# A decode attention block and its gradients: first wq chunk and third wo tile loaded at the turn between the passes, new homes for some gradient rows, another plan for the end

## The chip, the cores and the metric

The kernel runs on one core of a Trainium2 chip. The metric is the device time of one execution in microseconds; a comparison between two kernels is made from their medians. The core has five engines with a queue each: TensorE (PE, with its weight loads shown apart as PEld), VectorE (DVE), ScalarE (ACT), GpSimd (POOL) and SyncE (SP). Sixteen DMA engines move data between the device memory and the on-chip memory; transfers are issued from the queues of SP, ACT and POOL.

## The reference: what is computed

One token goes through an adaptive-layernorm block (a modulation vector made from `c` and `w_mod`), attention with a cache of 8192 keys and values for each of 32 heads of width 192, and a small mixer MLP. Then all gradients are taken with respect to ten of its inputs.

```python
mod = (_silu(c) @ w_mod).reshape(c.shape[0], 6, 1, -1)      # sa, ca, ga, sb, cb, gb
h = _layernorm(x) * (1 + ca) + sa
q = (h @ wq).reshape(B, Sq, Hq, Dh)                         # 640 -> 32 x 192
p = softmax(einsum(q, k) * Dh ** -0.5); o = einsum(p, v)
x = x + ga * (o @ wo)                                       # 6144 -> 640
h = _layernorm(x) * (1 + cb) + sb
x = x + gb * _B_ref(h, w1, w2, w3, w4)                      # w3: 640 x 1536, w4: 1536 x 640
out, vjp = jax.vjp(f, x, k_cache, v_cache, wq, wo, w3, w4, c, w_mod); grads = vjp(grad_out)
```

K and V are 100 MB each and are read (V twice), and their gradients dK and dV, 100 MB each, are written. Beside them stand the weights and their gradients: wq and dwq (640 x 6144), wo and dwo (6144 x 640), w_mod and its gradient (640 x 3840), and those of w3 and w4. All of these weight gradients are outer products of two vectors.

## The kernel before, in words

The forward pass runs over the heads: scores from K and q, softmax, the sums of V. It ends at about 530 us. Then comes the turn: the last head, the output projection, the MLP forward and backward, and the vector `dao`, from which the gradient of every head's output follows. The backward pass then runs 64 steps s = 0 to 63, two per head (half a head's 8192 positions each), from the last head down. A step multiplies a half of V by the head's gradient (DVE, L1094), sums over the width on PE (L1113), forms dS (L1459), writes dK (DVE, L1129) and dV (PE L1124, ACT L1125), and stores both from POOL (L1414, L1410), 1536 KB each. One half of V (1536 KB) is loaded per step from SP (L328), five steps ahead. dV and dK are built in a ring of five buffers (`OB`: KC, VB2, QT, KE, KD; QT is the memory of `qs_bc`), so each waits until the store five buffers earlier has landed; in the last steps V buffers that are no longer needed join the ring.

Every engine's order is the order of the program text: nothing is reordered. Into the 64 steps the smaller work is woven by a plan written by hand. `at(s0, n, g)` puts the next n pieces of a generator g at s0, s0 + 0.25, and so on; s0 is counted in steps, and each step has four slots (`slot()`, behind the second dV group, between the halves of dK, behind the sixth dV group, and at its end). At a slot every due piece is issued, in the order of the sorted plan. The pieces that matter here:

- `g_ld(n)` loads wo tile TL - n (TL = 15, 480 KB, L203) from SP into one of two buffers of tag `wo`. The load waits until the tile that had this buffer is finished, its store included.
- `g_do(n)` transposes that tile (two pieces, PE L903 and ACT L904, into the one buffer of tag `wT`) and forms the gradient of two heads' outputs (third piece, L1056). `g_dwo(n)` overwrites the tile with the rows of dwo (DVE, three instructions, L1257) and stores it from POOL.
- `g_dq(t)` and `g_wm(n)` work on chunks of wq and w_mod: a chunk is 960 KB and is worked on in two halves of five pieces (transposes, a small product, ten outer-product rows on DVE, L1216). The rows of the gradient overwrite the chunk, and the second half stores it (L1227). `next_w()` (L1154) loads the next chunk from SP in the last piece of a first half, in turn into `w_st` (the memory of `w4b`) and `stg`, one buffer each.
- `g_dw3(lo, n)` builds rows of the gradient of w3 in `stg` from `du_bc`, which lies in `w4b`, and stores them; `g_bcast` makes `dao_bc` and `du_bc`; `g_small` does small sums, one output among them.
- `put(out, w, hold)` stores at once or, for the two last wo tiles and the two last w_mod chunks, keeps the store back until a `g_held` piece (L1231).
- The twelve rows of the gradient of w4 (160 KB each) come from `dw4_act` (ACT, L962) and `dw4_dve` (DVE, L950) and are stored by `dw4_store` (POOL, L953), rows 0 to 4 from `dw4s` (part of `w4b`), the others from `stg`.

SP takes its waits in order too: while a load waits for its buffer, every load behind it stands. The order on SP at the turn is: V for s = 4, the eight-kilobyte load `er0` (L367), wo tile TL - 1, the second `er` load, then the two halves of V for s = 5 (L1424).

Of the kernel before, what the change touches and what calls it, by code (L numbers as in the profile page):

```python
# [20 lines left out]
def kernel(  # L21
# [1024 lines left out]
    stg0 = bst.tile([P, ND * CW], BF16, name="stg")  # L1046
# [19 lines left out]
    wo_l[TL - 1] = load_wo(TL - 1)  # L1066
# [11 lines left out]
    dw4_act(stg0, 5, 5, 6)  # L1078
# [6 lines left out]
    dw4_dve(stg0, 5, 6, 7)  # L1085
    dw4_store(stg0, 5, 2)
# [55 lines left out]
    cur = {}  # L1142
# [3 lines left out]
    def next_w():  # L1146
        if wseq:
            view, n = wseq.pop(0)
            if cur.setdefault("n", 0) % 2 == 0:
                w = wst.tile([P, ND, CW], BF16, name="w_st", tag="w", bufs=1)  # L1150
            else:
                w = bst.tile([P, ND, CW], BF16, name="stg")
# [32 lines left out]
    def g_chunk(b, first, v3, rows, dst, n, acc, lay):  # L1185
# [31 lines left out]
        if first:  # L1217
            next_w()
# [34 lines left out]
    def g_dwo(n):  # L1253
        t = TL - n
        w = wo_l.pop(t)
# [24 lines left out]

    def g_dw3(lo, n):
# [4 lines left out]
        if lo == 0:  # L1286
            dw4_dve(o3[:, n * F : n * F + D], 11, 11, 12)
            dw4_store(o3[:, n * F : n * F + D], 11, 1)
        nc.gpsimd.dma_start(out=dw3_v[:, lo : lo + n, :], in_=o3[:, 0 : n * F].rearrange("p (a r) -> p a r", a=n))
        if lo + n == ND:  # L1290
            next_w()
        yield
# [30 lines left out]
    at(2.0, 1, d)  # L1323
    at(2.25, 3, g_bcast(dao, ND, dao_bc))
    at(3.0, 1, g_dwo(0))
    at(4.75, 1, g_ld(2))
    d = g_do(2)
    at(6.0, 1, d)
    at(6.0, 2, d)
    at(6.5, 1, g_dwo(1))  # L1330
    at(6.75, 4, g_bcast(du, NF, du_bc))
    at(7.75, 1, g_dw3(0, 2))
    at(8.0, 1, g_ld(3))
    at(8.25, 2, g_small())
    at(8.75, 1, g_dwo(2))
    at(9.0, 3, g_do(3))
    at(9.75, 1, g_dw3(2, 2))
    at(10.0, 1, g_dwo(3))
    at(10.75, 1, g_ld(4))
    at(11.25, 1, g_dw3(4, 1))  # L1340
    at(13.0, 3, g_do(4))
    at(13.75, 1, g_dwo(4))
    for n in range(5, NT):
        d = DO0 + CWS * (n - 5) if n < NT - 2 else 47.75 + 0.75 * (n - NT + 2)
        at(d - 3.25, 1, g_ld(n))
# [3 lines left out]
    k, t = 0, TL  # L1349
    while t >= 0 or late:  # L1350
        if t >= 0 and not (late and k % 3 == 2):
            wseq.append((wq_v, t // 2))
            at(CW0 + CWS * k, 5, g_dq(t))
            at(CW0 + CWS * k + 1.25, 5, g_dq(t - 1))
            t -= 2
        else:
            wseq.append((wm_v, late[0]))
            at(CW0 + CWS * k, 10, g_wm(late.pop(0)))
        k += 1
    at(CW0 + CWS * k - 1.0, 2, g_finish_x())  # L1360
    for n in range(GX):
        wseq.append((wm_v, n))
        at(CW0 + CWS * k, 10, g_wm(n))
        k += 1
    at(CW0 + CWS * k - 1.0, 1, g_finish_c())
    for s0 in (60.25, 60.75, 61.25, 62.25):
        at(s0, 1, g_held())
# [58 lines left out]
    mul_q(0, 0)  # L1426
    load_v5(0, JQ)
# [19 lines left out]
    dw4_act(stg0, 5, 7, 11)  # L1447
# [4 lines left out]
    for s in range(NS):  # L1452
# [61 lines left out]
        if s == 0:  # L1514
            dw4_store(stg0[:, 2 * D : 6 * D], 7, 4)
# [60 lines left out]
```

## Time and profile before

| | |
|---|---|
| time, median of 3 runs | 1389.81 us (1385.27 to 1391.85) |
| the profiled execution: its own time | 1386.39 us |
| its span, first to last instruction | 1384.6 us |
| busy: PE, DVE, ACT, POOL | 83%, 80%, 66%, 8% |
| data moved by DMA | 569.38 MB |
| mean granted TensorE clock | 0.741 |

The profile is of one execution. A windows row gives start and end, its length, the busy time of PE, PEld, DVE, ACT and POOL with their counts of instructions, the granted TensorE clock (1 is full), the mean busy share of the 16 DMA engines, and the rate in GB/s. A row of a timeline gives the start, the duration, the engine (SPq is the DMA queue of SP), the line in the kernel, the operation, what is written and read, the count and, in brackets, how long the engine was idle before and what ended that. A row of a source line or tile gives the count, the least, median and largest duration in ns, and the first and last start. A waits row gives who waited for whom: total us, times, longest. The page's rows of DMA issues give the count, the size of one and the median time from issue to landing.

### The profile page before, as it was taken

What the parts mean: (1) busy time and instruction counts of PE and PEld (TensorE: products, weight loads), DVE (VectorE), ACT (ScalarE), POOL (GpSimd) and SP (SyncE); (2) the same over time, 40 slices, a digit from 0 to 9 for tenths busy, and PEclk for the clock granted to TensorE, in tenths of its full rate; (3) what the DMA queues carried; (4) which work ended last, traced back from release to release, by engine and by line L of the source; (5) the groups of instructions that cost most, each with busy time, mean ns of one, the idle gap of its engine ahead of it and who ended that gap; (6) DMA issues with size and microseconds to landing.
All of it is one profiled execution on the core that took longest, in us unless ns stands there. A gap on an engine that the chain in (4) does not pass through costs nothing.

```text
span 1384.6 us, 30509 instructions
## 1 busy us (share of the span) xinstructions
PE 1154.0 (83%) x12712; PEld 733.4 (53%) x12712; DVE 1109.2 (80%) x1455; ACT 911.1 (66%) x2007; POOL 108.6 (8%) x197
## 2 busy tenths in 40 slices
PE   3898989999998989987867977698778886987974
PEld 2777777777777777633323434343334442533421
DVE  4999999999999999986757677686677866876784
ACT  0777777777777778866545656576556665755754
POOL 0000000000000000111100111011101110110011
PEclk8999999999999999765556556565565555655555
DMA  9999999999999999799999999999999999999989
GB/s 383 396 423 425 424 416 423 413 426 418 424 413 425 415 414 380 252 416 424 422 422 425 426 414 426 426 419 425 426 422 425 417 426 384 419 425 426 422 365 378
DMA packets 76889, 569.38 MB, mean 411 GB/s; under 512 B 7439, under 2 KB 25215, under 8 KB 37199
## 3 DMA queue, kind: packets, MB, share of 16 engines
q1 hardware_dynamic: 51594, 342.03, 60.1%
q0 software_dynamic: 24640, 224.89, 38.7%
q8 instruction: 99, 1.62, 0.4%
q10 hardware_dynamic: 516, 0.51, 0.1%
q14 instruction: 40, 0.32, 0.1%
HBM read 340.97 MB, written 226.44 MB: 410 GB/s over the span
## 4 chain that ended last, share of the span: by engine, by line
issue 44%; DVE 25%; DMA 14%; PE 9%; POOL 5%; ACT 2%; POOLq 0%; SPq 0%; ACTq 0%; DVEq 0%
DVE prod L333 10%; DMA KB<-in_A_k_cache_dram 9%; DVE prod L337 5%; DVE vs L403 4%; DMA out_dram<-qs_bc 3%; PE mp L425 2%; POOL out_dram L1414 2%; POOL out_dram L1410 2%; PE half_ps L343 2%; DMA out_dram<-KB 1%; PE mp L430 1%; POOL out_dram L1227 1%; DVE pq L1094 1%; PE dot_ps L1113 1%; DVE S_h L347 1%
## 5 line engine op out<-in xcount | busy, mean ns | idle before, releaser
L1113 PE MATMUL dot_ps<-pq,ident_bf 128*128 128x256 bf16 x1494 | 365.1, 385 | 27.0 <-DVE dP L347 25.5
L410 ACT ACTIVATE vs<-VB,Ef 128x192 bf16<-128x192 bf16 x840 | 303.6, 447 | 0.0
L1125 ACT CAST KB<-dv_ps 128x768 bf16<-128x768 f32 x312 | 241.4, 805 | 83.5 <-PE dv_ps L1124 82.4
L1113 PEld LDWEIGHTS <-ident_bf 128*128 128x128 bf16 x1494 | 147.1, 121 | 172.8 <-issue 137.1
L333 DVE TENSOR_TENSOR prod<-KB,qs_bc 128x6144 bf16<-128x6144 bf16 x62 | 207.9, 3353 | 24.1 <-DMA KB<-in_A_k_cache_dram 16.6
L1124 PE MATMUL dv_ps<-do_r,er_b 1*128 1x192 bf16 x2016 | 220.9, 327 | 4.3 <-ACT KB L1125 2.8
L1129 DVE TENSOR_TENSOR KB<-qh,dS 128x3072 bf16<-128x3072 bf16 x74 | 128.1, 1753 | 95.3 <-DMA out_dram<-KB 76.4
L425 PE MATMUL mp<-vs,KB 128*128 128x193 bf16 x1984 | 188.6, 246 | 4.5 <-ACT vs L410 2.6
L425 PEld LDWEIGHTS <-KB 128*128 128x128 bf16 x1984 | 168.2, 97 | 13.6 <-DMA KB<-in_A_k_cache_dram 5.3
L904 ACT COPY wT<-wT_ps 128x1024 bf16<-128x1024 bf16 x82 | 79.2, 966 | 106.2 <-PE wT_ps L903 105.8
L1124 PEld LDWEIGHTS <-er_b 1*128 1x128 bf16 x2016 | 68.7, 103 | 141.2 <-issue 138.2
L343 PE MATMUL half_ps<-prod,ident_bf 128*128 128x256 bf16 x744 | 95.1, 279 | 44.0 <-DVE prod L337 43.9
L403 DVE TENSOR_TENSOR vs<-VB,E 128x1728 bf16<-128x1728 bf16 x120 | 123.7, 1052 | 0.3 <-ACT vs L410 0.3
L1094 DVE TENSOR_TENSOR pq<-VB,do_r 128x3072 bf16<-128x3072 bf16 x66 | 115.5, 1750 | 0.0
L337 DVE TENSOR_TENSOR prod<-prod 128x3072 bf16<-128x3072 bf16 x62 | 108.7, 1754 | 1.0
L1094 DVE TENSOR_TENSOR pq<-KB,do_r 128x3072 bf16<-128x3072 bf16 x62 | 108.5, 1750 | 0.0
L343 PEld LDWEIGHTS <-ident_bf 128*128 128x128 bf16 x744 | 72.8, 100 | 62.4 <-issue 53.5
L430 PE MATMUL mp<-vs,KB 128*64 128x193 bf16 x1968 | 105.7, 250 | 0.0
L1125 ACT CAST VB<-dv_ps 128x768 bf16<-128x768 f32 x96 | 74.7, 804 | 39.0 <-PE dv_ps L1124 38.7
L1125 ACT CAST qs_bc<-dv_ps 128x768 bf16<-128x768 f32 x104 | 80.1, 805 | 23.7 <-PE dv_ps L1124 23.2
L390 ACT ACTIVATE E<-S_h,negm 128x256 bf16<-128x256 f32 x31 | 15.7, 508 | 114.5 <-DVE negm L561 112.2
L430 PEld LDWEIGHTS <-KB 128*64 128x64 bf16 x1968 | 78.8, 109 | 19.8 <-issue 19.5
(380 smaller groups left out, 1209.4 us busy)
## 6 DMA issues: line engine op xcount, KB each, us to landing
VB<-in_A_v_cache_dram SPq DMA_DIRECT2D x93, 1536.0 KB
out_dram<-KB POOLq DMA_DIRECT2D x74, 1536.0 KB, 17.2
KB<-in_A_k_cache_dram SPq DMA_DIRECT2D x63, 1536.0 KB
KB<-in_A_v_cache_dram SPq DMA_DIRECT2D x29, 1536.0 KB
out_dram<-qs_bc POOLq DMA_DIRECT2D x25, 1536.0 KB, 17.9
out_dram<-VB POOLq DMA_DIRECT2D x25, 1536.0 KB, 17.7
wo_st<-in_A_wo_dram SPq DMA_DIRECT2D x31, 480.0 KB
w_st<-in_A_wq_dram SPq DMA_DIRECT2D x12, 960.0 KB
```

What stands on the lines that cost most here:

```text
L333: V_.tensor_tensor(out=prod, in0=src, in1=vec[:, None, :].to_broadcast([P, JH, DH]), op=ALU.mult)
L337: V_.tensor_tensor(out=prod[:, :, 0:HW], in0=prod[:, :, 0:HW], in1=prod[:, :, DH - HW : DH], op=ALU.add)
L343: T_.matmul(ps, lhsT=ident_bf, rhs=prod[:, :, k : k + TF], start=(k == 0), stop=(k == w - TF))
L403: V_.tensor_tensor(out=vs[:, 0:n, 0:DH].rearrange("p j (a b) -> p j a b", b=4), in0=v[:, v0 : v0 + n, :].rearrange("p j (a b) -> p j a b", ...
L410: A_.activation(out=vs[:, k, 0:DH], in_=v[:, v0 + k, :], func=ACT.Copy, scale=Ef[:, j0 + k : j0 + k + 1])
L425: T_.matmul(mp[:, 0:MW], lhsT=kb[:, j0 + k, 0:P], rhs=vs[:, k, 0:MW], start=(q == 0 and k == 0), stop=(z and k == JQ - 1), skip_group_chec ...
L430: T_.matmul(mp[p0 : p0 + 64, MO : MO + MW], lhsT=kb[:, j0 + k, P:DH], rhs=vs[:, k, 0:MW], start=False, stop=(z and k >= JQ - 2), skip_grou ...
L1094: V_.tensor_tensor(out=pq[:, q], in0=v_l[s][:, q * JQ : (q + 1) * JQ, :], in1=do_of(ht(s)[0])[:, None, :].to_broadcast([P, JQ, DH]), op=AL ...
L1113: T_.matmul(ps[:, q * JQ : (q + 1) * JQ, :], lhsT=ident_bf, rhs=pq[:, q, :, k : k + TS], start=(k == 0), stop=(k == w - TS), skip_group_ch ...
L1124: T_.matmul(ps[:, b, k * DH : (k + 1) * DH], lhsT=er[p0 : p0 + 1, 2 * m + k, :], rhs=doh[p0 : p0 + 1, :], start=True, stop=True)
L1125: A_.copy(out=dV4[:, 2 * q : 2 * q + 2, m * PW : (m + 1) * PW], in_=ps[:, :, 0:PW])
L1129: V_.tensor_tensor(out=dK[:, lo:hi, :].rearrange("p j (a b) -> p j a b", b=4), in0=qh.rearrange("p (a b) -> p a b", b=4)[:, None, :, :].to ...
```

## The change

It moves transfers and pieces of work; what is computed and how many bytes are moved stays as it is.

- Wo tile TL - 2 is loaded at the turn, right ahead of tile TL - 1; `g_ld(2)` is gone. So that its buffer is free, dwo(0) is built in `dw4s` and no longer in the tile TL.
- The first chunk of wq (chunk 7, for t = 15 and 14) is loaded into `stg` at the turn, on SP behind the second `er` load and ahead of the V halves for s = 5. It is worked on at steps 5.0 and 6.25 instead of 14.0 and 15.25. Its first half no longer loads the next chunk, since `stg` goes to dw3 first; the next load is made by the last dw3 piece, one slot behind it, into `w_st`. From there on the chunks alternate between the two buffers the other way round; chunks 1 to 9 keep their times.
- Rows 5 and 6 of the gradient of w4 are built in the buffer `wT`. Rows 7 to 10, on ACT in step 0 and stored in it, and row 11, in the first dw3 piece, are now five DVE rows in `dw4s` at steps 1.75 and 2.0, and one store of 800 KB.
- In the early steps do(2), the small sums, dwo(1), dwo(2) come earlier, and dwo(0), the broadcast of `du`, dw3 and do(3) later.
- Near the end do and dwo of tile n = 13 come half a step earlier; the load of tile n = 15 moves from 45.25 to 46.75, its work by half a step. Chunks 10, 11, 12 come 0.75, 0.5 and 0.25 step later, the two finishing pieces with them. The four held stores go out at 58.0, 58.0, 58.75 and 60.25 instead of 60.25, 60.75, 61.25 and 62.25.

```diff
...
     def do_of(h):
         return do_r[:, (TL - h // 2) % NDR, (h % 2) * DH : (h % 2 + 1) * DH]
 
-    stg0 = bst.tile([P, ND * CW], BF16, name="stg")
+    dw4t = bst.tile([P, 15 * P], BF16, name="wT", tag="wT")
     tp_pool.update(p=psT, t="t")
 
     def do_mm(t, b=None):
...
                 scale=rinv[:, h : h + 1],
             )
 
-    wo_l[TL - 1] = load_wo(TL - 1)
+    for t in (TL - 2, TL - 1):
+        wo_l[t] = load_wo(t)
     er_l = {0: er0, 1: load_er(1, nc.sync)}
 
     def q_bc(h, pool=psB, tag="b"):
...
 
     do_mm(TL, 1)
     dw4_store(dw4s[:, 4 * D : 5 * D], 4, 1)
-    dw4_act(stg0, 5, 5, 6)
+    dw4_act(dw4t, 5, 5, 6)
     h2b.append(psS.tile([P, 3], FP32, name="h2_pb", tag="s"))
     h2_part(2, ND)
     cx = bst.tile([P, HQ, ND], FP32, name="v_bc")
     V_.tensor_tensor(out=cx, in0=AO.rearrange("p k h -> p h k"), in1=dao[:, None, :].to_broadcast([P, HQ, ND]), op=ALU.mult)
     cs = ckS[:, 0:HQ]
     V_.reduce_sum(out=cs, in_=cx, axis=AX.X)
-    dw4_dve(stg0, 5, 6, 7)
-    dw4_store(stg0, 5, 2)
+    dw4_dve(dw4t, 5, 6, 7)
+    dw4_store(dw4t, 5, 2)
     qh = q_bc(H1, psT, "t")
     A_.copy(out=bo[:, 2:ND], in_=h2b[0])
 
...
     HEADS = ((0, 0, P, 0), (1, 0, 64, P), (2, 0, P, DH), (1, 64, P, DH + P))
     NWM = NMOD // CW
     GX = -(-2 * ND // 6)
-    cur = {}
+    cur = {"n": 1}
     held = []
     wseq = []
 
     def next_w():
         if wseq:
             view, n = wseq.pop(0)
-            if cur.setdefault("n", 0) % 2 == 0:
+            if cur["n"] % 2 == 0:
                 w = wst.tile([P, ND, CW], BF16, name="w_st", tag="w", bufs=1)
             else:
                 w = bst.tile([P, ND, CW], BF16, name="stg")
...
         for i in range(ND):
             V_.tensor_scalar(out=stg[:, i, :], in0=v_bc, scalar1=rows[:, i : i + 1], scalar2=None, op0=ALU.mult)
         if first:
-            next_w()
+            if n < HQ // 4 - 1 or dst is not dwq_v:
+                next_w()
         else:
             put(dst[:, :, lo : lo + CW], cur["w"], dst is dwm_v and n < GX)
         yield
...
 
     def g_dwo(n):
         t = TL - n
-        w = wo_l.pop(t)
+        w = wo_l.pop(t) if n else dw4s[:, 0 : 3 * D].rearrange("p (k a) -> p k a", k=3)
         for k in range(3):
             V_.tensor_scalar(out=w[:, k, :], in0=dao_bc, scalar1=o_col[:, 3 * t + k : 3 * t + k + 1], scalar2=None, op0=ALU.mult)
         put(dwo_v[t], w, t < 2)
...
         store_vec(x2, out_0[0], "x2")
         yield
 
+    def g_dw4():
+        dw4_dve(dw4s, 7, 7, 9)
+        yield
+        dw4_dve(dw4s, 7, 9, NF)
+        dw4_store(dw4s, 7, NF - 7)
+        yield
+
     def g_dw3(lo, n):
         dw3_v = out_6.rearrange("(i p) n -> p i n", p=P)
         o3 = bst.tile([P, ND, CW], BF16, name="stg").rearrange("p a r -> p (a r)")
         for i in range(n):
             V_.tensor_scalar(out=o3[:, i * F : (i + 1) * F], in0=du_bc, scalar1=n2[:, lo + i : lo + i + 1], scalar2=None, op0=ALU.mult)
-        if lo == 0:
-            dw4_dve(o3[:, n * F : n * F + D], 11, 11, 12)
-            dw4_store(o3[:, n * F : n * F + D], 11, 1)
         nc.gpsimd.dma_start(out=dw3_v[:, lo : lo + n, :], in_=o3[:, 0 : n * F].rearrange("p (a r) -> p a r", a=n))
+        yield
         if lo + n == ND:
             next_w()
-        yield
+            yield
 
     def g_finish_x():
         V_.tensor_copy(out=d_sa, in_=dha)
...
     d = g_do(1)
     at(1.25, 2, d)
     at(2.0, 1, d)
+    at(1.75, 2, g_dw4())
     at(2.25, 3, g_bcast(dao, ND, dao_bc))
-    at(3.0, 1, g_dwo(0))
-    at(4.75, 1, g_ld(2))
-    d = g_do(2)
-    at(6.0, 1, d)
-    at(6.0, 2, d)
-    at(6.5, 1, g_dwo(1))
-    at(6.75, 4, g_bcast(du, NF, du_bc))
-    at(7.75, 1, g_dw3(0, 2))
+    at(3.25, 3, g_do(2))
+    at(4.0, 2, g_small())
+    at(4.75, 1, g_dwo(0))
+    at(5.0, 5, g_dq(TL))
+    at(6.25, 5, g_dq(TL - 1))
+    at(5.75, 1, g_dwo(1))
+    at(7.5, 4, g_bcast(du, NF, du_bc))
     at(8.0, 1, g_ld(3))
-    at(8.25, 2, g_small())
-    at(8.75, 1, g_dwo(2))
-    at(9.0, 3, g_do(3))
-    at(9.75, 1, g_dw3(2, 2))
-    at(10.0, 1, g_dwo(3))
+    at(7.75, 1, g_dwo(2))
+    at(9.0, 1, g_dw3(0, 2))
+    at(9.75, 3, g_do(3))
+    at(10.5, 1, g_dw3(2, 2))
+    at(10.5, 1, g_dwo(3))
     at(10.75, 1, g_ld(4))
-    at(11.25, 1, g_dw3(4, 1))
+    at(12.0, 2, g_dw3(4, 1))
     at(13.0, 3, g_do(4))
     at(13.75, 1, g_dwo(4))
     for n in range(5, NT):
-        d = DO0 + CWS * (n - 5) if n < NT - 2 else 47.75 + 0.75 * (n - NT + 2)
-        at(d - 3.25, 1, g_ld(n))
+        d = DO0 + CWS * (n - 5) if n < NT - 3 else (44.0, 47.75, 49.0)[n - NT + 3]
+        at(d - (3.25 if n < NT - 1 else 2.25), 1, g_ld(n))
         at(d, 3, g_do(n))
         at(d + 0.75, 1, g_dwo(n))
     late = list(range(GX, NWM))
-    k, t = 0, TL
+    k, t = 1, TL - 2
+    wseq.append((wq_v, TL // 2))
+    cw = [CW0 + CWS * i for i in range(10)] + [49.75, 53.0, 56.25]
     while t >= 0 or late:
         if t >= 0 and not (late and k % 3 == 2):
             wseq.append((wq_v, t // 2))
-            at(CW0 + CWS * k, 5, g_dq(t))
-            at(CW0 + CWS * k + 1.25, 5, g_dq(t - 1))
+            at(cw[k], 5, g_dq(t))
+            at(cw[k] + 1.25, 5, g_dq(t - 1))
             t -= 2
         else:
             wseq.append((wm_v, late[0]))
-            at(CW0 + CWS * k, 10, g_wm(late.pop(0)))
+            at(cw[k], 10, g_wm(late.pop(0)))
         k += 1
-    at(CW0 + CWS * k - 1.0, 2, g_finish_x())
+    at(cw[k] - 0.75, 2, g_finish_x())
     for n in range(GX):
         wseq.append((wm_v, n))
-        at(CW0 + CWS * k, 10, g_wm(n))
+        at(cw[k], 10, g_wm(n))
         k += 1
-    at(CW0 + CWS * k - 1.0, 1, g_finish_c())
-    for s0 in (60.25, 60.75, 61.25, 62.25):
+    at(58.75, 1, g_finish_c())
+    for s0 in (58.0, 58.0, 58.75, 60.25):
         at(s0, 1, g_held())
     plan.sort(key=lambda p: p[0])
     NP = len(plan)
...
         nc.sync.dma_start(out=v_l[5][:, lo:hi, :], in_=V_hd[h5][:, t5 * JH + lo : t5 * JH + hi, :])
 
     mul_q(0, 0)
+    next_w()
     load_v5(0, JQ)
     half_q(0, 0)
     dv_groups(dV0, er, doh, (0, 2, 4, 6))
...
     dv_groups(dV0, er, doh, (1, 3, 5, 7))
     dv_store(0, dV0, JQ, JH)
     dw4_act(dw4s, 0, 3, 4)
-    dw4_act(stg0, 5, 7, 11)
     V_.memset(dha, 0.0)
     V_.memset(dsc, 0.0)
     row = None
...
         if s > 0 and late0:
             late0.pop(0)()
         dk_store(s, dK, JQ if s in (0, NS - 1) else 0, JH)
-        if s == 0:
-            dw4_store(stg0[:, 2 * D : 6 * D], 7, 4)
         if row is not None:
             dq_cols(row)
             row = None
```

## The prediction

> **What bounds the kernel now.** I read the page's busy line and its forty slices first, then the same stretches by windows, then the issue order on SP and POOL around every stretch where the DMA rate falls. The busy line and the slices:
>
> ```profile
> span 1384.6 us, 30509 instructions
> PE 1154.0 (83%) x12712; PEld 733.4 (53%) x12712; DVE 1109.2 (80%) x1455; ACT 911.1 (66%) x2007; POOL 108.6 (8%) x197
> DMA  9999999999999999799999999999999999999989
> GB/s 383 396 423 425 424 416 423 413 426 418 424 413 425 415 414 380 252 416 424 422 422 425 426 414 426 426 419 425 426 422 425 417 426 384 419 425 426 422 365 378
> DMA packets 76889, 569.38 MB, mean 411 GB/s; under 512 B 7439, under 2 KB 25215, under 8 KB 37199
> ```
>
> No engine is full over the span, and the DMA is full in nearly every slice: 569.38 MB at the 424 GB/s of a full slice would take 1343 us, and the span is 1384.6. So time is lost only where the DMA rate falls: the start, the middle (380, 252), one slice late (384) and the end (365, 378). The windows narrow that down; the last two numbers of a row are the DMA share and its rate:
>
> ```profile
> 554.00:560.00 6.00, 5.99 (x108) 5.40 (x106) 5.83 (x28) 5.25 (x7) 0.00 (x0) 1.00 0.04 11
> 560.00:562.00 2.00, 1.88 (x69) 1.79 (x65) 1.36 (x12) 1.97 (x3) 0.00 (x0) 1.00 0.74 246
> 565.00:566.00 1.00, 0.47 (x5) 0.24 (x2) 0.96 (x2) 1.00 (x4) 0.73 (x1) 0.50 0.01 5
> 566.00:574.00 8.00, 6.94 (x46) 4.36 (x46) 7.60 (x10) 7.10 (x12) 1.32 (x2) 0.50 0.93 281
> 574.00:584.00 10.00, 9.67 (x102) 6.58 (x100) 9.96 (x9) 8.01 (x12) 2.92 (x5) 0.73 1.03 415
> 584.00:600.00 16.00, 13.65 (x158) 7.76 (x158) 15.69 (x25) 13.72 (x23) 2.67 (x5) 0.89 1.00 387
> 600.00:1140.00 540.00, 433.75 (x3269) 208.05 (x3265) 382.30 (x559) 328.12 (x455) 61.17 (x108) 0.58 1.01 423
> 1168.00:1180.00 12.00, 4.59 (x35) 2.24 (x33) 11.19 (x23) 3.74 (x5) 1.11 (x2) 0.50 0.86 294
> 1180.00:1300.00 120.00, 104.77 (x796) 50.88 (x795) 88.36 (x133) 77.86 (x108) 12.67 (x22) 0.56 1.01 424
> 1300.00:1322.00 22.00, 18.87 (x144) 8.66 (x140) 14.13 (x22) 13.23 (x18) 1.60 (x3) 0.50 1.01 428
> 1322.00:1338.00 16.00, 12.37 (x78) 4.70 (x78) 14.90 (x21) 9.36 (x13) 3.19 (x6) 0.50 0.73 304
> 1338.00:1380.00 42.00, 25.92 (x167) 9.01 (x165) 28.16 (x23) 23.12 (x32) 6.59 (x11) 0.50 1.00 416
> ```
>
> Three holes lie in what the change touches: 554 to 574 (the turn from the forward to the backward pass), 1168 to 1180, and 1322 to 1338. Between them the DMA is full, so a byte taken out of a full stretch and put into a hole is worth its transfer time, and engine work that moves inside a full stretch is worth nothing as long as the DMA keeps a queue.
>
> **Part 1: the first wq chunk and the third wo tile go into the middle.** SP issues loads in order, so the place in its queue decides:
>
> ```profile
> 554.62 0.59 SPq L367 DMA_DIRECT2D qs_bc<-eT_d  x1
> 559.05 0.34 SPq L203 DMA_DIRECT2D wo_st<-in_A_wo_dram  x1
> 563.11 0.50 SPq L367 DMA_DIRECT2D er_b<-eT_d  x1
> 565.89 0.33 SPq L1424 DMA_DIRECT2D KB<-in_A_v_cache_dram  x1
> 578.54 0.76 POOL L953 DMA_DIRECT2D out_dram<-stg  x1
> ```
>
> The eight-kilobyte load at 554.62 is followed by an empty DMA until the wo load at 559.05; that load shows as traffic of 0.74 of 560 to 562, so bytes start some 1.4 us after the issue. The third wo tile (480 KB, 0.49 MB) is issued right behind 554.62, since the buffer of the tile TL is free once its transposes are done (the new dwo(0) writes into dw4s instead). At 424 GB/s it is 1.16 us, inside six empty microseconds: worth 1.16 whole. If the allocator hands the two tiles the other way round it goes at 559.4 and is still free.
>
> The wq chunk (960 KB, 0.98 MB, 2.32 us) stands in SP's order behind the er load of 563.11, so it is issued at about 563.7 and moves from 565.1. From there to 574 the idle share is 0.9 x 0.99 + 8 x 0.07 = 1.45 us; the rest of the chunk pushes V loads and stores that are moved there now. V5's two halves, next behind it on SP, still wait for a DVE product until 565.89, so SP holds nobody up if the chunk's buffer is free by then. I take 1.4; bounds 0 (it only pushes) and 2.32 (all of it absorbed, as 281 GB/s leaves room by bytes).
>
> The four w4 rows stored at 578.54 (640 KB, 1.55 us) leave and come back, with row 11, as one 800 KB store in s = 2. Both places are full (1.03 and 1.00): zero, and -1.55 if 578 to 584 falls dry without them. Part 1: **2.6 us**, bounds -0.4 and 3.5.
>
> The Trainium skill, "DMA: Bandwidth & Descriptors" (section on the anatomy of one DMA), speaks against this part: each DMA has a fixed cost of about 2.0 us beside bytes/436e3. By it the chunk would land at 563.7 + 2.0 + 2.3 = 568.0, which my 565.1 + 2.3 = 567.4 nearly is; an estimate that starts the bytes a full 2.0 us after the issue loses 0.6 of the idle time, and the sum below would be 7.6 instead of 8.2. The row at 559.05 shows the 1.4, so I keep it. The same page's specifications put the HBM limit of a core at about 358 GB/s, by which the 1.47 MB moved would be worth 4.1 us; the 423 to 428 of the full windows do not agree, and the measurement decides.
>
> **Part 2: engine work that moves.** Rows of one step s: 596.73 is dP of s = 3 and 1310.34 that of s = 58, 55 steps, 13.0 us each.
>
> ```profile
> 596.73 0.69 DVE L347 TENSOR_REDUCE dP<-dot_ps 128x32 f32<-128x512 f32 x1
> 1310.34 0.69 DVE L347 TENSOR_REDUCE dP<-dot_ps 128x32 f32<-128x512 f32 x1 [0.18 <-PE dot_ps L1113]
> L950 DVE TENSOR_SCALAR stg<-w4b,g__10309 x2: 377/378/380, 563.8 to 656.1; 128x640 bf16<-128x640 bf16 x2
> L962 ACT ACTIVATE stg<-w4b,g__10309 x5: 817/818/825, 564.0 to 577.2; 128x640 bf16<-128x640 bf16 x5
> 705.66 0.62 DVE L1285 TENSOR_SCALAR stg<-w4b,nQ 128x1536 bf16<-128x1536 bf16 x1 [2.78 <-DMA out_dram<-stg]
> out_dram<-stg POOLq DMA_DIRECT2D x6, 960.0 KB, 18.8
> ```
>
> Four ACT rows of 0.82 us go (3.3 us, in s = 0); four more DVE rows of 0.38 us come in s = 1.75 and 2.0 (1.5 us), where DVE is busy 15.69 of 16 us. That makes s = 2 later by 1.5 us, covered by the DMA that is full over the same 16 us; without that cover it costs 1.5. The two halves of chunk 7 (two of the dq groups, their transposes, POOL's 960 KB store) move from 14 to 5.0 and 6.25, do(2) from 6.0 to 3.25, dwo(0) from 3.0 to 4.75, the small sums from 8.25 to 4.0: all in a stretch at 423 GB/s, so zero. Behind them DVE, which is in order, meets stg three times: the dw3 steps at 9.0, 10.5 and 12.0 overwrite what was stored at 7.25, 9.0 and 10.5, 1.5 to 1.75 steps or 19.5 to 23 us before, against a landing of 18.8. Before, one such gap of 1.5 cost DVE 2.78 us and the DMA nothing. Zero, at most 3 x 2.8 if the DMA had no queue. In exchange next_w behind dw3 is a slot later, so SP no longer stands 10 us for it.
>
> **Part 3: the last wo tiles.** Where the DMA falls to 294 GB/s, SP had stood still:
>
> ```profile
> SPq L203 <- DMA out_dram<-wo_st: 40.7, 4, 23.8
> SPq L1154 <- DMA out_dram<-stg: 26.6, 5, 11.1
> 1145.32 0.33 SPq L328 DMA_DIRECT2D VB<-in_A_v_cache_dram  x1
> 1152.59 0.55 POOL L1227 DMA_DIRECT2D out_dram<-wo_st  x1 [9.59 <-DVE wo_st L1257]
> 1169.55 0.33 SPq L203 DMA_DIRECT2D wo_st<-in_A_wo_dram  x1
> 1169.97 0.92 SPq L328 DMA_DIRECT2D VB<-in_A_v_cache_dram  x1
> ```
>
> The load of the last wo tile and the store that empties its buffer stand in the same slot (45.25). SP reaches the load at 1145.7, the store goes out at 1152.59 and lands at 1169.5: 23.8 us with no load issued, and the next V load queued behind it. The queue runs dry: (424 - 294)/424 x 12 = 3.7 us of transfer time lost. With dwo(13) at 44.75 and the load at 46.75 the store goes out near 1140 and is down by 1158 (17 us as here), and SP comes to the load only behind the V load of s = 46, at about 1158. The wait is gone or some 2 us; the second row above shows that waits up to 11.1 us elsewhere left full windows. I take **3.5**, bounds 0 and 3.7. Next late at this place is the store queue, which is the full DMA again. The wq and wm chunks 10 to 12 move by 0.75, 0.5 and 0.25 step, within full stretches: zero. The load of the last one, at 54.0, meets a store put at 52.0; SP may wait some 5 us there, as it did in five places.
>
> **Part 4: the end.** When the last loads are through, the DMA lives on stores, and DVE makes them:
>
> ```profile
> 1319.79 1.76 DVE L1129 TENSOR_TENSOR qs_bc<-qh,dS 128x3072 bf16<-128x3072 bf16 x1 [6.71 <-DMA out_dram<-qs_bc]
> 1324.73 0.53 POOL L1414 DMA_DIRECT2D out_dram<-qs_bc  x1 [13.47 <-DVE dc_t L1308]
> 1362.29 0.56 POOL L1414 DMA_DIRECT2D out_dram<-VB  x1 [6.74 <-DVE VB L1129]
> ```
>
> ```profile
> L1231 POOL DMA_DIRECT2D out_dram<-wo_st x2: 545/545/545, 1337.3 to 1346.0; - x2
> L1231 POOL DMA_DIRECT2D out_dram<-stg x1: 886/886/886, 1346.5 to 1346.5; - x1
> L1231 POOL DMA_DIRECT2D out_dram<-w_st x1: 869/869/869, 1354.7 to 1354.7; - x1
> ```
>
> The chain starts when a store lands at 1319.6 and frees qs_bc, so it comes earlier by whatever parts 1 and 3 save. From there DVE runs without long waits to the last products, and from 1362.29 on six stores (two of 1536 KB, four of 768 KB: 6.3 MB, 14.8 us) remain. Counting every store as 1.4 us and its bytes at 424 GB/s, one behind the other, the 18 stores of before, from 1324.73 on (the six from 1362.29 are the last), end at 1380.6. The four held stores (the group above, 2.9 MB, 7.0 us) go out at 1337, 1346, 1346.5 and 1354.7, so some of them still stand ahead of the last six. At 58.0, 58.0, 58.75 and 60.25 they go out at about 1311, 1311, 1331 and 1341 and fill the hole at 1322 to 1338; the same count then has 1.5 us idle ahead of 1363.7 and ends at 1363.7 + 14.8 = 1378.5. Part 4: **2.1 us**. DVE sets it then, so no more than 2.1; not under 0, since the products that need VB and KD come later than the stores of these buffers land in the count.
>
> **Sum.** 2.6 + 3.5 + 2.1 = 8.2 us. The profiled execution (span 1384.6, own time 1386.39) would be 1376.4 and 1378.2. The median of the runs shown, 1389.81, stands 3.4 above that execution, and the answer is a median too: 1389.8 - 8.2 = **1381.6**, 0.6% less.
>
> **Rivals.** *The hole is not worth its bytes.* The loads of the middle only push what is moved there, and 578 to 584 falls dry (-0.4), the end gives nothing, the late wait goes (3.5): 1386.7. For it: 281 GB/s at a share of 0.93, so part of the middle is slow and not empty. Against it: 554 to 560 at 0.04. 0.10.
>
> *The late wait only moves.* If SP reaches the last wo load while the store of dwo(13) is under way after all, the dry stretch stays: 2.6 + 2.1, 1385.1. For it: chunk stores wait 18.8 us to land, and POOL may issue late, as at 1152.59 (9.59 us idle). Against: two whole steps lie between the slots instead of none. 0.07.
>
> *Slower: SP is held in the middle.* The chunk's load stands on SP ahead of every V load of the backward pass. Its buffer stg is a tile of the pool opened at the turn, first written by SP now instead of by ACT. If its memory is not free at 563.7, V5 and all behind it stand too; each V load that comes too late for a dry DMA is 1.57 MB, 3.7 us. The 6.8 us that the change has without the chunk are eaten by two loads; four, a hold to about 610, give +8.0 and 1397.8. For it: the er load before it, in the same pool, already waited until 563.11. Against it: ACT's rows on this pool's stg begin at 564.0. 0.15.
>
> **Numbers.** My forecast holds 0.68: 0.60 for more than 0.5% (7 us, about what a measurement of this kernel tells from no change) and 0.08 for less, since 8.2 is close to that bound. With the rivals: faster 0.60, same 0.08 + 0.10 + 0.07 = 0.25, slower 0.15. The range takes the upper bounds (3.5 + 3.7 + 2.1 = 9.3) and 5 us of spread of the runs shown (1385.27 to 1391.85) below, and both small rivals with some spread above: 1375.5 to 1389.0; the slower rival stays outside.
>
> **What would show it.** In the profile after: a wo load and a 960 KB load on SP between 555 and 565, and 554 to 566 no longer empty; V5 still issued at about 566 (later by 10 us or more is the slower rival); no wait of SP of 10 us or more on out_dram<-wo_st, and no window near 294 GB/s in the last third; the hole of 1322 to 1338 filled, and the last six stores with no held store ahead of them. It is wrong if DMA windows between 600 and 1300 fall under 415 GB/s, or if DVE's wait for out_dram<-stg in steps 9 to 12 leaves the DMA dry.

## The result and the profile after

The changed kernel takes 1386.12 us (median), the kernel before, on the same chip, 1388.32 us: a ratio of 0.9973, 95% interval 0.9960 to 0.9986, or 3.7 us less (1.9 to 5.6). The ratio is not the plain quotient of these two medians, which is 0.9984 or 2.2 us less. A second measurement, on a second occasion with its own runs of the kernel before (1387.61 against 1388.79), gave 0.9985 (0.9974 to 0.9997), 2.1 us less. So the change gains 2 to 4 us, some 0.2%, where 8.2 were forecast: the sign was right, the forecast time (1381.6) lies 4.5 us under the measured one, and 1386.12 is inside the range, which is 13.5 us wide. The forecast started from 1389.81, a median of three runs; from the 1388.32 measured beside the change, 8.2 less is 1380.1.

The profiled execution of the changed kernel has a span of 1386.1 us (its own time is 1387.89), 1.5 us more than the one shown of before. Single executions of one kernel differ by more than the effect, so the two are compared stretch by stretch. The page's first lines:

```profile
span 1386.1 us, 30498 instructions
PE 1177.9 (85%) x12712; PEld 739.7 (53%) x12712; DVE 1111.0 (80%) x1459; ACT 910.1 (66%) x2003; POOL 108.5 (8%) x196
DMA  9999999999999999799999999999999999999997
GB/s 382 389 415 415 419 423 425 407 426 421 421 415 423 406 421 384 286 413 423 422 424 419 422 410 428 425 420 426 422 408 421 417 423 422 397 420 417 424 416 336
DMA packets 76872, 569.38 MB, mean 411 GB/s; under 512 B 7422, under 2 KB 25198, under 8 KB 37182
```

The bytes are the same. The slice in the middle rose from 252 to 286, the one from 1144 to 1178 from 384 to 422 and the last but one from 365 to 416. But the one from 1178 to 1213 fell from 419 to 397, and the last from 378 to 336. Most windows of the prediction, and 562 to 565, for the changed kernel (DMA share and GB/s last):

```profile
554.00:560.00 6.00, 5.78 (x90) 5.46 (x88) 5.90 (x27) 5.31 (x10) 0.00 (x0) 1.00 0.41 157
562.00:565.00 3.00, 2.40 (x81) 2.23 (x78) 2.25 (x18) 2.96 (x6) 0.00 (x0) 0.89 0.54 164
565.00:566.00 1.00, 1.00 (x15) 0.95 (x16) 0.93 (x3) 0.35 (x4) 0.54 (x1) 0.50 0.07 16
566.00:574.00 8.00, 7.17 (x76) 5.17 (x74) 7.60 (x12) 7.03 (x13) 2.06 (x3) 0.50 0.88 296
574.00:584.00 10.00, 8.94 (x86) 5.57 (x83) 9.93 (x10) 5.36 (x9) 2.17 (x5) 0.63 1.00 405
600.00:1140.00 540.00, 455.35 (x3262) 213.75 (x3261) 382.21 (x557) 330.12 (x456) 61.51 (x108) 0.53 1.01 420
1168.00:1180.00 12.00, 3.90 (x27) 1.36 (x25) 6.22 (x9) 3.90 (x5) 1.11 (x2) 0.50 1.01 416
1180.00:1300.00 120.00, 104.11 (x803) 51.29 (x804) 92.72 (x145) 77.30 (x107) 12.61 (x22) 0.59 1.01 414
1300.00:1322.00 22.00, 18.93 (x152) 9.13 (x149) 13.40 (x20) 13.98 (x19) 2.66 (x5) 0.50 1.00 418
1322.00:1338.00 16.00, 12.45 (x79) 4.39 (x78) 15.36 (x22) 9.37 (x13) 3.45 (x6) 0.50 0.99 407
1338.00:1380.00 42.00, 26.55 (x169) 9.41 (x168) 28.97 (x25) 23.92 (x33) 5.25 (x10) 0.50 0.97 409
```

All three holes are smaller: 554 to 560 went from 11 to 157 GB/s, 1168 to 1180 from 294 to 416, 1322 to 1338 from 304 to 407. But 1180 to 1300 fell from 424 to 414, which over 120 us is 120 x 10/424 = 2.8 us of transfer time, nearly all of what 1168 to 1180 got back (12 x 122/424 = 3.5). And 1300 to 1322 and 1338 to 1380 each fell by 7 to 10. The holes were filled; part of them came out again elsewhere. The experiments ask which part of the change pays and where the rest goes.

SP's order in the middle is the one predicted, with V5 (L1433) right behind the chunk:

```profile
558.20 0.59 SPq L367 DMA_DIRECT2D qs_bc<-eT_d  x1
558.90 2.75 SPq L203 DMA_DIRECT2D wo_st<-in_A_wo_dram  x2
565.38 0.50 SPq L367 DMA_DIRECT2D er_b<-eT_d  x1
565.94 0.44 SPq L1155 DMA_DIRECT2D stg<-in_A_wq_dram  x1
568.17 2.99 SPq L1433 DMA_DIRECT2D KB<-in_A_v_cache_dram  x2
```

V5 goes out at 568.17, 2.3 us later than before (565.89). But the er load, which stands ahead of the chunk on SP, is as much later (563.11 there), so the chunk did not hold SP.

### The profile page after: what moved, and what is told of

Its sections match the earlier page's. It is cut to its first block, busy times and chain, and to the rows that moved or that the text cites. A ratio compares the mean times of both kernels' runs of the same rounds, so it can differ in the third digit from the quotient of the medians.

```text
span 1386.1 us, 30498 instructions
## 1 busy us (share of the span) xinstructions
PE 1177.9 (85%) x12712; PEld 739.7 (53%) x12712; DVE 1111.0 (80%) x1459; ACT 910.1 (66%) x2003; POOL 108.5 (8%) x196
## 4 chain that ended last, share of the span: by engine, by line
issue 41%; DVE 24%; DMA 16%; PE 10%; POOL 5%; ACT 2%; POOLq 0%; SPq 0%; DVEq 0%; ACTq 0%
DMA KB<-in_A_k_cache_dram 10%; DVE prod L333 10%; DVE prod L337 5%; DMA out_dram<-KB 4%; DVE vs L403 3%; PE mp L425 2%; DMA out_dram<-VB 2%; POOL out_dram L1423 2%; PE half_ps L343 2%; POOL out_dram L1419 2%; PE mp L430 1%; PE dot_ps L1114 1%; POOL out_dram L1229 1%; DVE pq L1095 1%; ACT vs L410 1%
## 5 line engine op out<-in xcount | busy, mean ns | idle before, releaser
L1114 PE MATMUL dot_ps<-pq,ident_bf 128*128 128x256 bf16 x1494 | 377.4, 395 | 32.7 <-DVE dP L347 29.1
L1125 PE MATMUL dv_ps<-do_r,er_b 1*128 1x192 bf16 x2016 | 226.7, 336 | 4.2 <-ACT KB L1126 2.9
```

The lines of the kernel that those rows point to most:

```text
L1114: T_.matmul(ps[:, q * JQ : (q + 1) * JQ, :], lhsT=ident_bf, rhs=pq[:, q, :, k : k + TS], start=(k == 0), stop=(k == w - TS), skip_group_ch ...
L1125: T_.matmul(ps[:, b, k * DH : (k + 1) * DH], lhsT=er[p0 : p0 + 1, 2 * m + k, :], rhs=doh[p0 : p0 + 1, :], start=True, stop=True)
```

## The experiments

The theory after the result: part 1 (the middle) pays, part 3 (the last wo tiles) and part 4 (the end) do not. All runs were timed against the kernel before on the same chip, on three occasions with a chip each; 0.001 of a ratio is 1.4 us. Gains are by these ratios; the quotient of the two medians differs from them by up to 2.1 us (the held stores alone: 0.8 us more by the ratio, 1.3 less by the medians), so a difference of 1 to 2 us settles nothing here.

**The middle alone.** The changed kernel, with the times of the last wo tiles, the late chunks and the held stores put back:

```
-        d = DO0 + CWS * (n - 5) if n < NT - 3 else (44.0, 47.75, 49.0)[n - NT + 3]
-        at(d - (3.25 if n < NT - 1 else 2.25), 1, g_ld(n))
+        d = DO0 + CWS * (n - 5) if n < NT - 2 else 47.75 + 0.75 * (n - NT + 2)
+        at(d - 3.25, 1, g_ld(n))
-    cw = [CW0 + CWS * i for i in range(10)] + [49.75, 53.0, 56.25]
+    cw = [CW0 + CWS * i for i in range(14)]
-    at(cw[k] - 0.75, 2, g_finish_x())
+    at(cw[k] - 1.0, 2, g_finish_x())
-    at(58.75, 1, g_finish_c())
-    for s0 in (58.0, 58.0, 58.75, 60.25):
+    at(cw[k] - 1.0, 1, g_finish_c())
+    for s0 in (60.25, 60.75, 61.25, 62.25):
```

> The change without its end: the old load and work times of the last wo tiles, the old chunk times and the old times of the held stores. Theory of the holes (each part is worth what its DMA hole held): 2.6 us faster than before, 1385.7 against 1388.3, with the SP wait of some 24 us at the last wo load and the dry stretch behind it still there, and the hole ahead of the last steps too. Rival (the middle is not worth its bytes, since the full stretches behind it give it back): within 1 us of before. In its trace 554 to 566 should carry the two new loads in both cases; the theories differ in when step 10 and step 40 are reached, counted from the load of V for s = 5.

Measured: 0.9983 (0.9969 to 0.9997), 2.4 us less than before. The prediction's term was 2.6. The sign in the trace that the expectation names does not show the gain: from V5's load to dP of s = 10 (dP is written by one DVE row in every step, L347) it takes 117.9 us where the kernel before takes 116.3 (the work on the first wq chunk now lies ahead of it), and to dP of s = 40 it takes 522.8 against 516.2. These are two single executions, so the same times for all kernels stand at the end of the next experiment.

**The third wo tile alone.** The kernel before with one load moved:

```
-    wo_l[TL - 1] = load_wo(TL - 1)
+    for t in (TL - 2, TL - 1):
+        wo_l[t] = load_wo(t)
-        w = wo_l.pop(t)
+        w = wo_l.pop(t) if n else dw4s[:, 0 : 3 * D].rearrange("p (k a) -> p k a", k=3)
-    at(4.75, 1, g_ld(2))
```

> The kernel before with only one edit: the third wo tile is loaded at the turn, and the first dwo is written into the free w4 rows. The prediction's term for it is 1.16 us, its bytes at 424 GB/s: ratio about 0.9992. If all of the middle's 2.4 us came from this load (and the wq chunk only pushed): 0.9983. If it only pushes what follows: 1.000 or more.

Measured: 0.9994 (0.9978 to 1.0010), 0.8 us less; the interval takes in zero and the predicted 1.16. The stretch of the turn in one window (before, then this kernel, then the middle alone, then the changed kernel):

```profile
554.00:574.00 20.00, 17.80 (x266) 14.15 (x264) 18.58 (x58) 17.60 (x29) 2.59 (x4) 0.71 0.49 150
```

```profile
554.00:574.00 20.00, 17.58 (x269) 14.37 (x267) 18.45 (x58) 17.42 (x30) 2.59 (x4) 0.74 0.55 169
```

```profile
554.00:574.00 20.00, 17.80 (x279) 14.75 (x280) 18.54 (x66) 17.50 (x30) 2.59 (x4) 0.73 0.61 206
```

```profile
554.00:574.00 20.00, 18.35 (x287) 15.30 (x285) 18.57 (x67) 17.54 (x32) 2.60 (x4) 0.76 0.63 215
```

The rates over 20 us give 0.38, 1.12 and 1.30 MB more than before, or 0.9, 2.6 and 3.1 us at 424 GB/s, beside measured gains of 0.8 and 2.4 for the first two. All eight profiles with the new middle have 205 to 221 here, the four with the old one 146 to 171. So it is settled that more bytes move at the turn; their split between tile and chunk rests on 169, which lies inside the scatter of the old ones. In the spans of the profiled executions it does not show: they are 1384.6 to 1387.4 in the four with the old middle and 1382.9 to 1390.2 in the seven whole kernels with the new one, since a single execution scatters by more than the effect. From 554 to 820 the eight with the new middle move 402 GB/s in the mean, the four with the old one 399 (266 x 3/424 = 1.9 us); from 820 to 1140, where the code is the same, all of them move 415 to 423, and that scatter alone is worth 6 us. Counted from V5's load, the eight reach dP of s = 25 after 312.0 us in the mean, the four after 315.5; but dP of s = 40 after 518.7 and 518.5. From s = 25 to 40 the eight take 204.8 to 209.4 us, the four 201.7 to 204.0. So in the traces the lead is there at s = 25 and gone at s = 40, as the rival has it that full stretches behind give the gain back. The 2.4 us rest on the times alone; what happens between s = 25 and 40 was not tried.

**The last wo tiles alone.** The kernel before with the new times of wo tiles 13 to 15 and of the late chunks (the lines marked + and - the other way round, above), the held stores as before:

> Before, with only the new times of the wo tiles 13 to 15 and of the chunks 10 to 12; held stores at their old times. Theory of the holes: 3.5 us faster (no SP wait over 11 us at the last wo load, no window near 294 GB/s). Rival (the dry stretch was worth only its idle DMA share, 12 x 0.14 = 1.7 us, the low rate there belonging to the transfers): 1.7 us faster or less.

Measured: 0.9993 (0.9975 to 1.0011), 1.0 us less where 3.5 were expected. The interval just reaches 3.5, so this time alone does not exclude the forecast; the rival's "1.7 or less" is inside. No run has the new wo times without the new chunk times, so the two are not told apart.

**The held stores alone.** The kernel before with one line:

```
-    for s0 in (60.25, 60.75, 61.25, 62.25):
+    for s0 in (58.0, 58.0, 58.75, 60.25):
```

> Before, with only the four held stores at 58.0, 58.0, 58.75 and 60.25. Theory of the holes: 2.1 us faster, the hole at 1322 to 1338 filled, the last six stores with no held store ahead. Rival (the end belongs to the chain of DVE, which the early stores hold up: the buffer of dV of s = 58 is free later): 0 to 1 us faster or slower, with a wait of DVE for out_dram<-VB of 1 us or more at s = 60 that before does not have.

Measured: 1.0006 (0.9989 to 1.0023), 0.8 us more where 2.1 less were expected. The interval reaches to 1.5 less, not to 2.1. The hole filled (402 GB/s from 1322 to 1338, 304 before). The rival's time fits, but its sign does not: VectorE has no wait for VB at s = 60 in this trace, and dP of s = 59 to dP of s = 63 takes 33.95 us, as before.

**Both ends together.** The kernel before with the new wo times and the early held stores:

> Before, with the new times of wo tiles, chunks and held stores together, and nothing of the middle. Theory of the holes: 3.5 + 2.1 = 5.6 us faster. Rival of the cheap dry stretch and the held-up chain: 1.7 + 0 = 1.7 us faster. If the parts do not add up, the sum of the two runs alone differs from this one.

Measured: 0.9984 (0.9965 to 1.0002), 2.2 us less where 5.6 were expected, 4.9 at the most by the interval. Part 3 and part 4 together are the term that fell.

**The held stores back.** The changed kernel with part 4 taken out. From here on theory A says that the chain of VectorE products sets the tail, and theory B that the DMA's bytes do:

```
-    for s0 in (58.0, 58.0, 58.75, 60.25):
+    for s0 in (60.25, 60.75, 61.25, 62.25):
```

> The changed kernel with the four held stores back at their old times (60.25, 60.75, 61.25, 62.25). Theory A (the chain of VectorE products sets the tail from s = 57 on, and the early held stores only get ahead of the store that frees VB): about 1 us less than the changed kernel, ratio to the kernel before about 0.996 to 0.998; VectorE's wait of 1.15 us for VB at s = 60 goes, and the time from dP of s = 59 to dP of s = 63 falls from 35.2 to about 34.0 us. Theory B (the prediction: the hole of 1322 to 1338 is worth the bytes of the held stores): 2.1 us more than the changed kernel, ratio to before about 0.999.

Measured: 0.9981 (0.9967 to 0.9995), between the two measurements of the changed kernel. The wait for VB went and dP of s = 59 to dP of s = 63 fell to 33.9 us, as theory A had it, but no gain in time is shown: 0.9981 is at the edge of theory A's 0.996 to 0.998, and the interval takes in theory B's 0.999 too.

**No held stores.** The changed kernel, with the four stores not made:

```
         if hold:
-            held.append((out, w))
+            pass
-    for s0 in (58.0, 58.0, 58.75, 60.25):
-        at(s0, 1, g_held())
```

> The changed kernel without the four held stores at all (two wo gradient tiles and two wm chunks, 2.9 MB, 7.0 us at 424 GB/s, are not written). Theory A (VectorE's chain sets the tail): 1 to 3 us less than the changed kernel, from VB's wait of 1.15 us and a shorter drain; the time from dP of s = 59 to dP of s = 63 about 34.0 us, and from dP of s = 63 to the end 20 to 22 us as now. Theory B (the DMA's bytes set the tail): 6 to 7 us less than the changed kernel.

Measured: 0.9941 (0.9918 to 0.9965), 8.2 us less than before and 4.5 to 6 less than the changed kernel. From dP of s = 57 to the end it takes 79.1 us, where the changed kernel takes 85.5: 2.9 MB taken away are worth 4.5 to 6 us of their 7.0 by the times, 6.4 by this stretch. That is near theory B's 6 to 7 and well over theory A's 1 to 3, so theory A, as I had put it, falls: bytes count in the tail. But moving them to an earlier place showed no gain. The end of this kernel:

```profile
1322.00:1338.00 16.00, 14.30 (x90) 5.15 (x88) 14.99 (x23) 11.07 (x15) 2.71 (x5) 0.50 0.96 363
1360.00:1364.00 4.00, 3.41 (x27) 1.27 (x24) 3.93 (x5) 3.82 (x6) 1.06 (x2) 0.50 0.48 202
1364.00:1376.00 12.00, 2.18 (x19) 0.90 (x15) 2.30 (x2) 3.84 (x6) 1.06 (x2) 0.50 1.00 418
1376.00:1380.00 4.00, 0.00 (x0) 0.00 (x0) 0.00 (x0) 0.00 (x0) 0.00 (x0) 0.50 0.53 221
```

Here DVE is busy 3.93 of 4 us at 1360 to 1364 while the DMA is half idle: with 7 us of bytes less, DVE's chain is the bound. It is the floor of the tail, and the changed kernel is above it.

**The last wo load later.** Theory C says that the rest of SP's wait makes the slow stretch behind 1180, theory D that it does not:

```
-        at(d - (3.25 if n < NT - 1 else 2.25), 1, g_ld(n))
+        at(d - (3.25 if n < NT - 1 else 1.25), 1, g_ld(n))
```

> The changed kernel with the load of the last wo tile one step later (47.75 for 46.75), so that the store that frees its buffer has landed when SP gets to it. Theory C (the rest of SP's wait, 11.2 us at 1175, is what makes the slow stretches of 1185 to 1205, 355 to 395 GB/s where 424 was): SP's longest wait on a wo store falls under 3 us, 1185 to 1205 comes back to 410 to 424 GB/s, and the time falls by about 2 us. Theory D (the slow stretches are not of that wait): wait gone, time and rate unchanged within 1 us.

Measured: 0.9959 (0.9942 to 0.9975), 2.0 us under the first measurement of the changed kernel, though the intervals overlap. Its trace speaks against theory C: SP's long wait on a wo store is gone, yet the slow stretch is still there, earlier and deeper:

```profile
1168.00:1180.00 12.00, 3.46 (x25) 1.08 (x22) 6.32 (x10) 3.63 (x5) 1.11 (x2) 0.50 0.96 398
1185.00:1195.00 10.00, 9.96 (x84) 4.91 (x82) 7.66 (x13) 6.16 (x10) 1.86 (x3) 0.50 0.97 335
1168.00:1210.00 42.00, 31.04 (x217) 14.63 (x215) 29.14 (x45) 22.44 (x31) 4.29 (x7) 0.50 0.99 398
```

**The same with other held times, and the changed kernel once more**, three kernels side by side. The one with the held stores behind the store that frees VB:

```
-        at(d - (3.25 if n < NT - 1 else 2.25), 1, g_ld(n))
+        at(d - (3.25 if n < NT - 1 else 1.25), 1, g_ld(n))
-    for s0 in (58.0, 58.0, 58.75, 60.25):
+    for s0 in (58.75, 58.75, 60.25, 61.25):
```

> The changed kernel with the last wo load one step later (47.75) and the held stores at 58.75, 58.75, 60.25 and 61.25, so that the two wo gradients go out behind the store that frees VB and not ahead of it. Theory A (early held stores lose what they gain through VB's wait and through a late last packet): VectorE has no wait for VB at s = 60, dP of s = 59 to dP of s = 63 is about 34.0 us, the hole of 1322 to 1338 is still filled, and the time is 1 to 2 us under the kernel with the last wo load later alone (ratio to before about 0.995). If the held stores' place does not matter: the same time as that kernel within 1 us. If the hole is worth its bytes early: 1 to 2 us more.

The second has the same first edit, and 60.25, 60.75, 61.25, 62.25 for the held stores:

> The changed kernel with the last wo load one step later (47.75) and all held stores at their old times (60.25 to 62.25). Theory A: about 1 us less than the kernel with the last wo load later alone, no wait for VB, last packets ending within about 1 us of each other, and the hole of 1322 to 1338 back. Theory B (hole worth its bytes): 2 us more than that kernel. If the old and the new places cost the same (each loses what it gains): within 1 us.

> The changed kernel itself, beside the two others on one chip. Expected: ratio 0.997 to 0.998 to the kernel before, as measured at first (0.9973); a wait of about 1 us for VB at s = 60 as in its first profile; a slow stretch below 400 GB/s within 1185 to 1205. If the kernel with the last wo load later is really faster (Theory C), the two others lie 1.5 us or more under this one; if its 2 us were chance (Theory D), all three lie within 1 us.

Measured: 0.9988 (0.9973 to 1.0002), 0.9975 (0.9961 to 0.9989) and 0.9985 (0.9974 to 0.9997). The wait for VB is gone in the first two (34.0 us in both from dP of s = 59 to dP of s = 63), without a gain over the changed kernel beside them in the first and with at most 1.4 us in the second. The third has its wait for VB (1.1 us) and its slow stretch (377 GB/s from 1185 to 1205) again. Against the kernel with the last wo load later alone (0.9959, on another occasion) the first two are 4.0 and 2.2 us slower, so no theory gets its number here; that kernel was not timed a second time. All seven measurements of whole kernels with the new middle (the one without held stores left out) lie between 0.9959 and 0.9988, with a mean of 0.9978; the middle alone is 0.9983. No edit of the end stands out of that, and none of these kernels is shown to beat the changed one.

## Why the prediction was right in sign and wrong in size

**Part 1 (2.6 us) agrees with the measured time.** 2.4 us were measured for the middle alone (0.4 to 4.3), and the trace of the turn shows 2.6 to 3.1 us more of bytes moved; that the traces lose the lead again by s = 40 stays open. One reading of this part was wrong. The wo load of 559.05 lies whole inside the window from 560 to 562 (246 GB/s x 2 us = 0.49 MB), so that window's share does not say when its bytes start. They start some 1.0 us after the issue, not 1.4:

```profile
559.50:560.00 0.50, 0.50 (x24) 0.50 (x24) 0.50 (x5) 0.49 (x2) 0.00 (x0) 1.00 0.00 0
560.00:560.50 0.50, 0.50 (x27) 0.50 (x24) 0.50 (x6) 0.47 (x2) 0.00 (x0) 1.00 0.86 177
```

That adds at most 0.4 us to the sum. The prediction's other estimate, by which a fixed 2.0 us loses 0.6 us, is inside the same interval. The Trainium skill, "DMA: Bandwidth & Descriptors" (section on the anatomy of one DMA), gives that fixed cost for transfers issued from GpSimd and puts most of it behind the last byte, so bytes that start 2.0 us after the issue do not follow from it. These runs do not tell the three sums apart.

**Part 2 (zero) held as far as the traces show.** 574 to 584 did not fall dry (405 after 415). From 560 to 800 VectorE's waits for out_dram<-stg are 3.7 us in two places, one of 2.8 us before, and the window from 600 to 1140 has 420 where 423 was. That difference is within the scatter of that stretch (417 to 423 over all thirteen profiles).

**Part 3 (3.5 us) was the term mis-sized most: 1.0 us measured alone (1.5 more to 3.5 less), 0.3 us by the traces.** "The wait is gone or some 2 us" was wrong. The store of dwo(13) went out at 1148.86 and not near 1140:

```profile
1148.86 0.55 POOL L1229 DMA_DIRECT2D out_dram<-wo_st  x1
```

and the last wo load still waited for it, 11.2 us at the longest:

```profile
SPq L203 <- DMA out_dram<-wo_st: 14.0, 2, 11.2
```

But the larger error is the price. A dry stretch read off one execution was taken for the cost of SP's wait. Over 1168 to 1210, the kernel before and the changed one:

```profile
1168.00:1210.00 42.00, 33.03 (x282) 17.48 (x281) 36.30 (x62) 27.43 (x40) 4.82 (x8) 0.65 0.97 387
```

```profile
1168.00:1210.00 42.00, 31.15 (x248) 15.48 (x247) 30.66 (x46) 24.00 (x34) 4.28 (x7) 0.59 1.00 400
```

This window holds the dry stretch and what follows it. The four profiled kernels with the old wo times have 387, 401, 413 and 399 there, all with SP's wait of 22 to 24 us; the nine with the new times have 398 to 410, with waits of 12 us down to 1.4. The means are 400 and 403: 42 x 3/424 = 0.3 us, small beside the scatter. Before's 387 was the lowest of all thirteen, and it was the one shown. From dP of s = 44 to dP of s = 57 the means are 166.8 and 166.6 us. Within that stretch the thirteen show a gain and a loss of nearly the same size. From 1168 to 1180 the four have 353 GB/s in the mean and the nine 415: 12 x 62/424 = 1.8 us gained, half of the 3.7 that the one execution gave. From 1185 to 1205, where the kernel before and the changed one have

```profile
1185.00:1205.00 20.00, 19.13 (x132) 9.86 (x130) 15.16 (x27) 14.88 (x23) 2.65 (x4) 0.57 1.01 422
```

```profile
1185.00:1205.00 20.00, 19.29 (x146) 9.41 (x145) 14.79 (x19) 13.72 (x21) 2.65 (x4) 0.56 1.00 383
```

the four have 422 to 426, 424 in the mean, and the nine 375 to 402, 387 in the mean: 20 x 37/424 = 1.7 us lost again. So the loss behind the old dry stretch belongs to the new times of wo tiles and chunks and is no scatter. The prediction had put the moved chunks at zero; whether they or the wo tiles bring the loss is not shown.

What is late next is shown by the kernel whose last wo load does not wait. SP's waits from 1160 to 1190 (us in total, times, longest), then what VectorE did, then SP's next load:

```profile
SPq L328 <- DVE pq L1095: 31.9, 2, 20.6
```

```profile
1173.68 3.43 DVE L1130 TENSOR_TENSOR KB<-qh,dS 128x3072 bf16<-128x3072 bf16 x2 [11.41 <-DMA out_dram<-KB]
...
1182.76 1.75 DVE L1095 TENSOR_TENSOR pq<-KB,do_r 128x3072 bf16<-128x3072 bf16 x1
```

```profile
1184.53 0.33 SPq L328 DMA_DIRECT2D KB<-in_A_v_cache_dram  x1
```

VectorE stands 11.41 us, until 1173.68, for a gradient store to land and free an output buffer. Behind it on the in-order engine are the two products pq that read the V buffer, the second until 1184.5, and SP's next V load, at 1184.53, has waited 20.6 us for them: nearly as long as SP stood for the wo store in the kernel before. In the changed kernel, where SP stood 11.2 us for the wo store, the same V load went out at 1184.64, so that wait did not set it. Before, VectorE had the same kind of wait (8.3 us), hidden beside SP's. So the rival "the late wait only moves" is nearer to what happened than the forecast, though through another wait than it named: not the store of dwo(13) alone, but the ring of V and output buffers. Why the DMA then runs at 335 to 400 GB/s with a share near 1.00 is left open; no run isolates it.

**Part 4 (2.1 us) showed no gain.** The steps as far as VectorE were right: the held stores went out at 1314, 1330 and 1338, the hole at 1322 to 1338 filled, and VectorE set the last six stores. Two things were not in the count. "The products that need VB and KD come later than the stores of these buffers land" failed: with two wo stores ahead of it, VB's store landed late, and VectorE has a new wait, the number in brackets in this row:

```profile
1342.26 3.43 DVE L1130 TENSOR_TENSOR VB<-qh,dS 128x3072 bf16<-128x3072 bf16 x2 [1.15 <-DMA out_dram<-VB]
```

Four of the five kernels with the stores at 58.0 have this wait (1.1 to 1.3 us); the held stores alone have none and gained nothing either, so the wait is not the whole of it. And the DMA engines do not finish together. The changed kernel, then before:

```profile
1380.00:1382.00 2.00, 0.00 (x0) 0.00 (x0) 0.00 (x0) 0.00 (x0) 0.00 (x0) 0.50 0.22 89
1382.00:1384.00 2.00, 0.00 (x0) 0.00 (x0) 0.00 (x0) 0.00 (x0) 0.00 (x0) 0.50 0.06 25
```

```profile
1380.00:1382.00 2.00, 0.00 (x0) 0.00 (x0) 0.00 (x0) 0.00 (x0) 0.00 (x0) 0.50 0.57 237
1382.00:1384.00 2.00, 0.00 (x0) 0.00 (x0) 0.00 (x0) 0.00 (x0) 0.00 (x0) 0.50 0.01 6
```

A share of 0.06 is one sixteenth, as much as one of the 16 engines gives. By the packet records, the last 16 packets end over 3.0 us in the changed kernel and over 0.5 to 1.4 us in the six kernels with the old held times; in the six with earlier ones it is 1.9 to 3.0, also where VB no longer waits, and without held stores 0.1. From dP of s = 57 to the end, the five kernels with the stores at 58.0 take 84.8 us in the mean, the six with the old times 84.8 too. The same account by bytes: what each kernel moves in that time (381 and 385 GB/s over 84.6 and 85.5 us), at 424 GB/s, leaves 8.6 us before and 7.9 in the changed kernel. So of the 3.9 us by which the hole was filled (16 x 103/424) 0.7 is left. Behind 1380 the changed kernel loses 5.6 us of transfer time where 3.4 was, and from 1338 to 1380 0.7 more, with a dip at 1362 to 1366 (356 and 207 GB/s in its two halves). The uneven finish is the largest part of what came back. The Trainium skill, "DMA: Bandwidth & Descriptors" (section on why a DMA increments its semaphore by 16), says that a DMA runs on up to 16 engines which finish independently; the 3.0 us between the last packets agree, and a count of bytes alone leaves it out. What makes one engine late wasn't tried, so that the early stores cause it is a comparison of twelve kernels and not more.

**The sum.** 2.6 + 3.5 + 2.1 was to be 8.2; the parts measured alone are 2.4 + 1.0 - 0.8 = 2.6 us, and the whole 3.7 and 2.1. Of the rivals, "the hole is not worth its bytes" forecast 3.1 us less, nearest to the measured gain, but by luck: it had the late wait give 3.5 and the middle nothing. "SP is held in the middle" did not happen. The prediction had named its own sign of being wrong, a window between 600 and 1300 under 415 GB/s: 1180 to 1300 has 414. And its "no wait of SP of 10 us or more on out_dram<-wo_st" did not come true: 11.2.

## What to carry to other kernels

A hole in the DMA can be worth its bytes where next to nothing is in flight (11 GB/s at the turn: 2.4 us came, 0.4 to 4.3, where 2.6 were forecast). Where a stall belongs to a closed loop of loads, products and stores through a few buffers, taking away the wait that ends last bares the next one: look what else was waiting in that same stretch, and price it by the mean rate over the whole loop's stretch and several executions, not by the dip of one. At the end of a kernel, look when the last packets end and not only when the bytes would be through: here their spread went from 0.9 to 3.0 us.

## What the runs showed that was not expected

- A DMA share near 1.00 does not mean full rate: 10 us at a share of 0.97 moved 335 GB/s (1185 to 1195, the kernel with the last wo load later), beside 426 at a share of 1.01 from 1140 to 1160.
- With the same bytes stored earlier the last 16 packets end over 1.9 to 3.0 us (six kernels) where it was 0.5 to 1.4 (six kernels), and without held stores 0.1.
- Eight profiled kernels with the same code for the turn issue V5 between 566.0 and 569.1 us, as far apart as the change is worth. Two profiles can't settle such a change; rates over one stretch in thirteen could.
